# Layer norms of a two-layer kernel: eps on VectorE, one power first, additions behind the normalizations, a new order of phases

## The chip, the cores and the metric

The kernel runs on one core of a Trainium2 chip. The metric is the device time of one execution in microseconds; the median of three runs of the kernel before is 268.06 us (267.25 to 268.32).

## The reference, cut to what matters

An attention layer A and an MLP-mixer layer B, one after the other, each inside a layer norm and a residual. S is 2048, D is 448, F is 1792.

```python
def _layernorm(x, eps=1e-5):
    return (x - mean(x)) / jnp.sqrt(var(x) + eps)

def _A_ref(x, wqkv, wo):            # 16 heads of 28, window of 8 keys, dilation 2
    q, k, v = split(x @ wqkv)
    logits = einsum("bhsd,bhswd->bhsw", q, k[idx]) * scale
    attn = softmax(where(mask, logits, -1e9))
    return einsum("bhsw,bhswd->bhsd", attn, v[idx]) @ wo

def _B_ref(x, w1, w2, w3, w4):
    h = gelu(_layernorm(x) @ w1)
    hs = concat(quarters of h shifted by -1, +1, -2, +2 rows) @ w2
    x1 = x + hs
    return x1 + gelu(_layernorm(x1) @ w3) @ w4

h  = x + _A_ref(_layernorm(x), wqkv, wo)
h2 = h + _B_ref(_layernorm(h), w1, w2, w3, w4)
```

## The kernel before, in words

The 2048 rows are worked in four blocks of 512 (t = 0 to 3), each of four tiles of 128 rows (il). The phases of a block are:

- N1: row statistics of the input on VectorE, the reciprocal root of variance plus eps on GpSimd, four normalizations on VectorE into a tile of `lntm`. This is norm kind 0.
- A1: 16 transposes on TensorE, evicted by ScalarE (`transposed`, line 422), and 48 matmuls for q, k and v.
- A2: four VectorE multiplications of q with shifted k (tile `qk_r`), 32 small matmuls that sum over a head (four run at a time), and the softmax on VectorE and ScalarE (`mx`, `ls`, `zs`, `rz`, `pb`). The weights are written to a scratch tensor in DRAM.
- A3: 16 DMAs read them back, broadcast over the partitions of each head (tile `av_r`, four buffers, 28 partitions of 8192 bytes by each DMA). Four VectorE multiplications with shifted v follow, 32 accumulating matmuls, the projection with wo and the residual (20 matmuls), and ScalarE's write back into `xin`.
- B1: two layer norms in one (kind 1). The first norm's factor `rs_y[0:4]` is needed by B2; the product of both, `rs_y[4:8]`, is what B1 normalizes with. Then transposes, w1 and GELU. `mrs` is mean times factor and is needed by B3 alone.
- B2: w2 on the shifted quarters (it needs the neighbouring blocks' B1), the residual into `xb` in f32, statistics, kind 2's root, four normalizations in f32. Behind each normalization a GpSimd addition puts `xin` onto the same row tile of `xb` (line 538 and the following).
- W3: 14 x 4 matmuls with GELU into `h3T` tiles. B3: 4 x 14 matmuls, a VectorE step that adds `xb` (`ost`), and the output DMA. "w3" in the list is the load of the W3 weights, which lie in the place of wqkv, so that it follows A1 3.

The order is not written into the phases. `PLAN` (line 13) lists phases by priority. Each operation is recorded by `add` (line 99) with its priority, an assumed duration and what it reads and writes. `schedule` (line 140) then places the operations: on each engine, of those ready within a small slack of the earliest, the one with the best priority, and so on, with buffers given out as they come free. Each engine then runs its own list in that fixed order (`emit_engine`, line 608; every instruction is issued at line 612). SP's queue issues all DMAs in its own fixed order too. `rstd` (line 403) holds the root's steps, `normalize` (line 418) one normalization.

Of the kernel before, what the change touches and what calls it, by code (L numbers as in the profile page):

```python
# [9 lines left out]
F32 = mybir.dt.float32  # L10

_LAST = {}
PLAN = "N1 0, A1 0, N1 1, A2 0, N1 2, A1 1, A3 0, B1 0, A2 1, A1 2, N1 3, A2 2, A1 3, A3 1, A3 2, B1 1, B2 0, w3 0, B1 2, A2 3, W3 0, A3 3, B1 3, B3 0, B2 1, W3 1, B2 3, B3 1, B2 2, W3 2, B3 2, W3 3, B3 3"


class _Pool:


    def __init__(self, name, view, n):
        self.name = name; self.view = view  # L20
        self.free = [(0.0, k, ()) for k in range(n)]


# [65 lines left out]
class _Sched:  # L89
# [6 lines left out]
        self.prio = 0  # L96
        self.live = {}

    def add(self, eng, meth, dur, lag=60.0, chan=None, nbytes=0, table=None, **kw):
        op = _Op(len(self.ops), self.prio, eng, meth, kw, float(dur), float(lag))  # L100
        op.table = table
        if chan is not None:
            op.is_dma = True; op.chan = chan; op.nbytes = nbytes
        reads, writes = [], []
        for k, v in kw.items():
            if isinstance(v, _View):
                if v.tile not in op.tiles:
                    op.tiles.append(v.tile); v.tile.left += 1; v.tile.ops.append(op)
                name, plo, phi, ivs, psum = _rects(v.ap(0))
                name = v.tile.key  # L110
            elif isinstance(v, bass.AP):
                name, plo, phi, ivs, psum = _rects(v)
            else:
                continue
            if psum:
                plo, phi, ivs = 0, 128, [(0, 1)]
            (writes if k in self.WRITE_KEYS else reads).append((name, plo, phi, ivs))
        pe = eng == "pe"
        for (sp, plo, phi, ivs) in reads:
            for e in self.live.setdefault(sp, []):  # L120
                if e[1] and e[2] < phi and plo < e[3] and any(e[4] < hi and lo < e[5] for lo, hi in ivs):
                    op.deps.add(e[0])
        for (sp, plo, phi, ivs) in writes:
            L = self.live.setdefault(sp, [])
            for e in L:
                if e[2] < phi and plo < e[3] and any(e[4] < hi and lo < e[5] for lo, hi in ivs):
                    (op.odeps if pe and e[1] and e[0].eng == "pe" else op.deps).add(e[0])
            L[:] = [e for e in L if not (plo <= e[2] and e[3] <= phi
                                         and any(lo <= e[4] and e[5] <= hi for lo, hi in ivs))]
        for (sp, plo, phi, ivs) in reads:  # L130
            self.live[sp].extend([op, False, plo, phi, lo, hi] for lo, hi in ivs)
        for (sp, plo, phi, ivs) in writes:
            self.live[sp].extend([op, True, plo, phi, lo, hi] for lo, hi in ivs)
        op.deps.discard(op); op.odeps.discard(op)
        self.ops.append(op)
        return op
# [3 lines left out]
    def schedule(self, dma_bw=190.0, dma_fixed=2000.0, table_load=1300.0):  # L140
# [18 lines left out]
        table = None  # L159
        for _ in range(n):  # L160
            best = None
            for e in engs:
                fr = free[e]
                cands = []
                for op in ready[e]:
                    st = max(rdy[op.idx], fr)
                    for t in op.tiles:
                        if t.slot is None:
                            if not t.pool.free:
                                st = None  # L170
                                break
                            st = max(st, min(t.pool.free)[0])
                    if st is not None:
                        cands.append((st, op))
                if not cands:
                    continue
                first = min(st for st, _ in cands)
                st, op = min((c for c in cands if c[0] <= first + self.SLACK[e]), key=lambda c: (c[1].prio, c[1].idx))
                if best is None or st < best[0]:
                    best = (st, op)  # L180
            if best is None:
                stuck = sorted((op.prio, op.idx, op.eng, op.meth, [t.key for t in op.tiles])
                               for e in engs for op in ready[e])
                raise RuntimeError("no instruction can be placed: %s" % stuck[:20])
            st, op = best
            ready[op.eng].remove(op)
            for t in op.tiles:
                if t.slot is None:
                    f = min(t.pool.free)
                    t.pool.free.remove(f)  # L190
                    t.slot = f[1]; t.before = f[2]
                op.deps.update(t.before)
            op.t0 = st
            if op.is_dma:
                free[op.eng] = st + op.dur
                dma_free = max(st + op.dur, dma_free) + op.nbytes / dma_bw
                op.t1 = dma_free + dma_fixed
            else:
                dur = op.dur
                if op.table is not None and op.table != table:  # L200
                    table = op.table; dur += table_load
                free[op.eng] = st + dur
                op.t1 = st + dur + op.lag
            for t in op.tiles:
                t.left -= 1
                if t.left == 0:
                    t.pool.free.append((max(o.t1 for o in t.ops), t.slot, tuple(t.ops)))
            order[op.eng].append(op)
            self.gorder.append(op)
            for ch in children[op.idx]:  # L210
                npend[ch.idx] -= 1
                rdy[ch.idx] = max(rdy[ch.idx], op.t1 if op in ch.deps else op.t0)
                if npend[ch.idx] == 0:
                    ready[ch.eng].append(ch)
# [52 lines left out]
def bass_sequential_preLN__sliding_local_dilated__mixer_s_mlp__prompt_kernel(  # L267
# [30 lines left out]
    with ExitStack() as es:  # L298
# [50 lines left out]
        def shifted(t, u, c):  # L349
            return bass.AP(AR, A_KV + t * KVB + (u * 4 + c) * KVW + PADK, [[A_END, KC], [64, 8], [-DIL, NW], [1, 64]])  # L350

        def mm(out_ap, lhsT, rhs, start, stop, n, share=1.0):
            return S.add("pe", "matmul", 2.5 + share * n / 2.4, 220.0, out=out_ap, lhsT=lhsT, rhs=rhs, start=start, stop=stop)
        def act(out_ap, in_ap, func, n, **kw):
            table = {ACT.Exp: "exp", ACT.Gelu_apprx_tanh: "gelu"}.get(func)
            return S.add("act", "activation", 185 + 0.82 * n, 80.0, table=table, out=out_ap, in_=in_ap, func=func, **kw)
        def dve(meth, n, mode=1.0, **kw):
            return S.add("dve", meth, (90 + n / mode) / 0.96, 120.0, **kw)
        def pool(meth, n, **kw):
            return S.add("pool", meth, 130 + n / 0.5, 60.0, **kw)  # L360
        def dma(chan, out_ap, in_ap, nbytes, dur=400.0):
# [36 lines left out]

        def ln_stats(kind, src_ap, i):
            dve("bn_stats", D, out=st6[:, i, :], in_=src_ap)  # L400
            dve("bn_aggr", 8, out=mv[:, kind, i, :], in_=st6[:, i, :])

        def rstd(kind, t):


            var4 = mv[:, kind, 4 * t:4 * t + 4, 1]
            n = 8 if kind == 1 else 4
            pool("tensor_scalar", 4, out=rs_x[:, kind, t, 0:4], in0=var4, scalar1=EPS, scalar2=None, op0=ALU.add)
            if kind == 1:
                pool("tensor_scalar", 4, out=rs_x[:, kind, t, 4:8], in0=var4, scalar1=1.0 + EPS, scalar2=EPS * EPS,  # L410
                     op0=ALU.mult, op1=ALU.add)
            S.add("pool", "tensor_tensor", 1000, 60.0, out=rs_y[:, kind, t, 0:n], in0=rs_x[:, kind, t, 0:n],
                  in1=mhalf[:, 0:n], op=ALU.pow)
            if kind == 1:
                pool("tensor_tensor", 4, out=mrs[:, t, :], in0=mv[:, 1, 4 * t:4 * t + 4, 0], in1=rs_y[:, 1, t, 0:4],
                     op=ALU.mult)

        def normalize(kind, t, il, col, out_ap, in_ap):
            dve("tensor_scalar", D, 2.0, out=out_ap, in0=in_ap, scalar1=mv[:, kind, 4 * t + il, 0:1],
                scalar2=rs_y[:, kind, t, col:col + 1], op0=ALU.subtract, op1=ALU.mult)  # L420

        def transposed(ln):
# [115 lines left out]
        def phase_B2(t):  # L538
# [8 lines left out]
                ln_stats(2, xb[t][:, il, :], i)  # L547
            rstd(2, t)
            ln = _Tile(P_ln)
            for il in range(4):  # L550
                i = 4 * t + il
                normalize(2, t, il, il, ln(lambda v, il=il: v[:, il, :]), xb[t][:, il, :])
                pool("tensor_tensor", D, out=xb[t][:, il, :], in0=xb[t][:, il, :], in1=xin[:, i, :], op=ALU.add)
            b2_a[t] = transposed(ln)

        h3 = {}
# [1 line left out]
        def phase_W3(t):  # L558
            a = b2_a[t]
            h3[t] = [_Tile(P_h3) for _ in range(NF)]  # L560
            for f in range(NF):
                b = _Tile(P_bank)
                for c in range(4):
                    mm(b(), w3_s[:, c, f * 128:(f + 1) * 128], a(lambda v, c=c: v[:, c, :]), c == 0, c == 3, 512)
                act(h3[t][f](), b(), ACT.Gelu_apprx_tanh, 512)

        def phase_B3(t):
# [86 lines left out]
```

## Time and profile before

| what | value |
|---|---|
| median of 3 runs | 268.06 us (267.25 to 268.32) |
| span of the profiled execution | 269.7 us |
| TensorE busy | 241.8 us |
| VectorE busy | 167.5 us |
| ScalarE busy | 112.8 us |
| GpSimd busy | 54.3 us |

The profile has one execution. Its span is the only time recorded of it; the median is that of other executions. Matmuls are pipelined and their ends are modelled, so that neighbouring rows overlap a little. PEclk is the granted TensorE clock as a share of 2.4 GHz: 1.00 is the full level, 0.50 is 1.2 GHz.

### The profile page before, as it was taken

What the parts mean: (1) busy time and instruction counts of PE and PEld (TensorE: products, weight loads), DVE (VectorE), ACT (ScalarE), POOL (GpSimd) and SP (SyncE); (2) the same over time, 40 slices, a digit from 0 to 9 for tenths busy, and PEclk for the clock granted to TensorE, in tenths of its full rate; (3) what the DMA queues carried; (4) which work ended last, traced back from release to release, by engine and by line L of the source; (5) the groups of instructions that cost most, each with busy time, mean ns of one, the idle gap of its engine ahead of it and who ended that gap; (6) DMA issues with size and microseconds to landing.
All of it is one profiled execution on the core that took longest, in us unless ns stands there. A gap on an engine that the chain in (4) does not pass through costs nothing.

```text
span 269.7 us, 3248 instructions
## 1 busy us (share of the span) xinstructions
PE 241.8 (90%) x1297; PEld 125.6 (47%) x1297; DVE 167.5 (62%) x234; ACT 112.8 (42%) x178; POOL 54.3 (20%) x87
## 2 busy tenths in 40 slices
PE   0599897998899999798489999999899998999995
PEld 0355352453445565354154555555345544445452
DVE  3449999589896998888877553354992243001122
ACT  1222663353254944240238771314277035612600
POOL 5102042004306000303913000031761026000000
PEclk9999998699799999889959999999999999999999
DMA  7990003999599679995006992010000110000201
GB/s 217 307 328 16 2 1 53 174 174 174 114 165 175 124 193 187 158 159 91 0 19 142 181 186 38 17 38 17 0 0 2 34 34 2 0 0 0 71 17 51
DMA packets 24367, 24.70 MB, mean 92 GB/s; under 512 B 1376, under 2 KB 23456, under 8 KB 24352
## 3 DMA queue, kind: packets, MB, share of 16 engines
q1 hardware_dynamic: 24352, 24.50, 43.7%
q8 instruction: 10, 0.16, 0.3%
q14 instruction: 5, 0.04, 0.1%
HBM read 22.13 MB, written 2.36 MB: 91 GB/s over the span
## 4 chain that ended last, share of the span: by engine, by line
PE 66%; DVE 20%; POOL 7%; ACT 3%; issue 1%; DMA 1%
PE ps L612 66%; DVE st L612 5%; DVE lntm L612 4%; POOL rs_y L612 4%; DVE av_r L612 3%; POOL rs_x L612 2%; ACT actT L612 2%; DVE qk_r L612 2%; DVE mv L612 2%; DMA xin<-in_A_x_dram 1%; DVE arena L612 1%; ACT xin L612 1%; DVE zs L612 1%; DVE ls L612 1%; DVE pb L612 1%
## 5 line engine op out<-in xcount | busy, mean ns | idle before, releaser
L612 PE MATMUL ps<-actT,arena 112*128 112x512 bf16 (+1 forms) x416 | 100.8, 395 | 2.2 <-ACT actT L612 2.2
L612 PEld LDWEIGHTS ps<-actT,arena 112*128 112x128 bf16 (+1 forms) x416 | 47.9, 118 | 48.4 <-issue 7.7
L612 ACT ACTIVATE actT<-ps 112x1024 bf16<-112x1024 bf16 (+1 forms) x40 | 32.8, 852 | 69.0 <-PE ps L612 69.0
L612 ACT ACTIVATE arena<-ps 112x512 bf16<-112x512 f32 x58 | 33.7, 599 | 31.7 <-PE ps L612 31.2
L612 ACT ACTIVATE h3T<-ps 128x512 bf16<-128x512 f32 x56 | 32.1, 599 | 33.8 <-PE ps L612 33.7
L612 PE MATMUL ps<-arena,h3T 128*128 128x448 bf16 x224 | 44.4, 352 | 0.0
L612 DVE SCALAR_TENSOR_TENSOR ost<-ps,mrs,arena 128x448 bf16<-128x448 f32 x16 | 10.7, 681 | 52.8 <-PE ps L612 52.3
L612 DVE TENSOR_TENSOR av_r<-av_r,arena 112x4096 bf16<-112x4096 bf16 x16 | 36.4, 2285 | 9.1 <-DMA av_r<-attn_p_scratch 9.1
L612 POOL TENSOR_SCALAR rs_x<-mv 128x4 f32<-128x4 f32 x16 | 11.3, 706 | 141.8 <-DVE mv L612 141.5
L612 PE MATMUL ps<-av_r,ident 112*112 112x512 bf16 x128 | 33.1, 411 | 6.2 <-DVE ls L612 4.6
L612 DVE TENSOR_TENSOR qk_r<-arena 112x4096 bf16<-112x4096 bf16 x16 | 36.0, 2279 | 0.0
L612 PEld LDWEIGHTS ps<-arena,h3T 128*128 128x128 bf16 x224 | 21.8, 98 | 20.0 <-ACT h3T L612 0.2
L612 PE MATMUL ps<-ident,lntm 128*112 128x128 bf16 x192 | 18.9, 238 | 10.3 <-DVE lntm L612 10.1
L612 PEld LDWEIGHTS ps<-av_r,ident 112*112 112x112 bf16 x128 | 17.8, 141 | 19.4 <-DVE ls L612 5.0
L612 DVE BATCH_NORM_STATS2 st<-xin 128x6 f32<-128x448 bf16 x32 | 19.3, 604 | 11.2 <-ACT xin L612 6.7
L612 PEld LDWEIGHTS ps<-ident,lntm 128*112 128x112 bf16 x192 | 15.3, 142 | 19.2 <-DVE lntm L612 16.0
L612 POOL TENSOR_TENSOR rs_y<-rs_x,mhalf 128x4 f32<-128x4 f32 (+1 forms) x12 | 18.7, 1562 | 1.0
L612 POOL TENSOR_TENSOR arena<-arena,xin 128x448 f32<-128x448 f32 x16 | 18.0, 1154 | 2.5 <-DVE lntm L612 2.5
L612 PE MATMUL ps<-wo_s,actT 112*128 112x448 bf16 x64 | 16.4, 353 | 1.4 <-ACT actT L612 1.4
L612 PE MATMUL ps<-actT,w_s 112*112 112x512 bf16 x64 | 16.7, 412 | 0.8 <-ACT actT L612 0.8
L612 DVE TENSOR_SCALAR lntm<-xin,mv,rs_y 128x448 bf16<-128x448 bf16 x32 | 10.6, 392 | 7.1 <-POOL rs_y L612 7.1
L612 DVE TENSOR_SCALAR lntm<-arena,mv,rs_y 128x448 bf16<-128x448 f32 x16 | 12.9, 866 | 2.5 <-POOL rs_y L612 2.4
(38 smaller groups left out, 126.6 us busy)
## 6 DMA issues: line engine op xcount, KB each, us to landing
av_r<-attn_p_scratch SPq DMA_DIRECT2D x64, 224.0 KB
arena<-in_B_w_dram SPq DMA_DIRECT2D x2, 1568.0 KB, 9.9
xin<-in_A_x_dram SPq DMA_DIRECT2D x4, 448.0 KB, 8.5
out_dram<-ost SPq DMA_DIRECT2D x16, 112.0 KB, 1.7
arena<-in_A_wqkv_dram SPq DMA_DIRECT2D x1, 1176.0 KB, 7.3
w_s<-in_B_w_dram SPq DMA_DIRECT2D x2, 392.0 KB, 9.5
attn_p_scratch<-pb SPq DMA_DIRECT2D x4, 128.0 KB, 1.7
wo_s<-in_A_wo_dram SPq DMA_DIRECT2D x1, 392.0 KB, 10.8
```

What stands on the lines that cost most here:

```text
L612: inst = getattr(eng, op.meth)(**op.kw)
```

## The change

The list of phases is rewritten. The addition of eps (for kind 1 also the product form of the second norm) goes from GpSimd to VectorE. For kind 1 the power over eight columns becomes two over four, and the one that B1's normalizations need is issued first. The GpSimd additions of B2 depend on all four normalizations of the block (`after`). Some assumed durations are changed (`ns`, the power's 1100). `P_h3.order` gives the `h3T` buffers out in order of their use, and the first matmul of each W3 tile holds its buffer (`hold`). The diff, cut to its core:

```diff
-PLAN = "N1 0, A1 0, N1 1, A2 0, N1 2, A1 1, A3 0, B1 0, A2 1, A1 2, N1 3, A2 2, A1 3, A3 1, A3 2, B1 1, B2 0, w3 0, B1 2, A2 3, W3 0, A3 3, B1 3, B3 0, B2 1, W3 1, B2 3, B3 1, B2 2, W3 2, B3 2, W3 3, B3 3"
+PLAN = "N1 0, A1 0, N1 1, A2 0, A3 0, N1 2, A1 1, A2 1, A3 1, A1 2, N1 3, A2 2, B1 0, B1 1, B2 0, A1 3, A3 2, w3 0, A2 3, W3 0, B1 2, B2 1, B3 0, A3 3, B1 3, B2 2, W3 1, B3 1, B2 3, W3 2, B3 2, W3 3, B3 3"
...
-    def add(self, eng, meth, dur, lag=60.0, chan=None, nbytes=0, table=None, **kw):
+    def add(self, eng, meth, dur, lag=60.0, chan=None, nbytes=0, table=None, after=(), hold=None, **kw):
...
+        op.deps.update(after)
...
+        if hold is not None:
+            op.tiles.append(hold); hold.left += 1; hold.ops.append(op)
...
+                            if t.pool.order and t.pool.order[0] is not t:
+                                st = None
+                                break
...
-            dve("bn_aggr", 8, out=mv[:, kind, i, :], in_=st6[:, i, :])
+            dve("bn_aggr", 8, ns=180.0, out=mv[:, kind, i, :], in_=st6[:, i, :])
...
             var4 = mv[:, kind, 4 * t:4 * t + 4, 1]
-            n = 8 if kind == 1 else 4
-            pool("tensor_scalar", 4, out=rs_x[:, kind, t, 0:4], in0=var4, scalar1=EPS, scalar2=None, op0=ALU.add)
+
+            def power(lo):
+                S.add("pool", "tensor_tensor", 1100, 60.0, out=rs_y[:, kind, t, lo:lo + 4], in0=rs_x[:, kind, t, lo:lo + 4],
+                      in1=mhalf[:, 0:4], op=ALU.pow)
+
             if kind == 1:
-                pool("tensor_scalar", 4, out=rs_x[:, kind, t, 4:8], in0=var4, scalar1=1.0 + EPS, scalar2=EPS * EPS,
-                     op0=ALU.mult, op1=ALU.add)
-            S.add("pool", "tensor_tensor", 1000, 60.0, out=rs_y[:, kind, t, 0:n], in0=rs_x[:, kind, t, 0:n],
-                  in1=mhalf[:, 0:n], op=ALU.pow)
+                dve("tensor_scalar", 4, out=rs_x[:, kind, t, 4:8], in0=var4, scalar1=1.0 + EPS, scalar2=EPS * EPS,
+                    op0=ALU.mult, op1=ALU.add)
+                power(4)
+            dve("tensor_scalar", 4, out=rs_x[:, kind, t, 0:4], in0=var4, scalar1=EPS, scalar2=None, op0=ALU.add)
+            power(0)
...
-            dve("tensor_scalar", D, 2.0, out=out_ap, in0=in_ap, scalar1=mv[:, kind, 4 * t + il, 0:1],
+            return dve("tensor_scalar", D, ns=450.0 if kind == 2 else 330.0, out=out_ap, in0=in_ap, scalar1=mv[:, kind, 4 * t + il, 0:1],
...
+            nz = [normalize(2, t, il, il, ln(lambda v, il=il: v[:, il, :]), xb[t][:, il, :]) for il in range(4)]
             for il in range(4):
                 i = 4 * t + il
-                normalize(2, t, il, il, ln(lambda v, il=il: v[:, il, :]), xb[t][:, il, :])
-                pool("tensor_tensor", D, out=xb[t][:, il, :], in0=xb[t][:, il, :], in1=xin[:, i, :], op=ALU.add)
+                pool("tensor_tensor", D, after=nz, out=xb[t][:, il, :], in0=xb[t][:, il, :], in1=xin[:, i, :], op=ALU.add)
...
+            P_h3.order.extend(h3[t])
...
-                    mm(b(), w3_s[:, c, f * 128:(f + 1) * 128], a(lambda v, c=c: v[:, c, :]), c == 0, c == 3, 512)
+                    mm(b(), w3_s[:, c, f * 128:(f + 1) * 128], a(lambda v, c=c: v[:, c, :]), c == 0, c == 3, 512,
+                       hold=h3[t][f] if c == 0 else None)
```

## Rows read from the trace of the kernel before

**Rows 1.** The page's first line: the span.

```profile
span 269.7 us, 3248 instructions
```

**Rows 2.** Stages: from:to, length, busy us of each engine, granted clock, DMA share, GB/s.

```profile
70.00:90.00 20.00, 19.39 (x123) 10.64 (x122) 17.35 (x22) 11.50 (x19) 4.23 (x4) 0.95 0.94 166
...
42.38:142.16 99.78, 89.12 (x481) 46.95 (x482) 85.62 (x98) 43.22 (x69) 21.72 (x18) 0.90 0.74 132
142.16:266.89 124.73, 121.69 (x649) 61.82 (x647) 51.44 (x87) 53.23 (x87) 21.88 (x26) 1.00 0.20 44
```

**Rows 3.** Waits of TensorE from 42.3 to 142.16 us: total, times, longest.

```profile
PE ps L612 <- DVE ls L612: 4.6, 1, 4.6
...
PE ps L612 <- DVE lntm L612: 2.6, 3, 1.2
```

**Rows 4.** The chain that ended last, through B1 1 and B2 0: start, us, what.

```profile
106.08 0.55 ACT xin L612
...
122.12 0.69 DVE arena L612
...
123.47 2.19 DVE av_r L612
...
125.84 2.19 POOL rs_x L612
...
128.10 2.93 POOL rs_y L612
...
131.06 3.21 DVE lntm L612 x4
```

**Rows 5.** Waits of TensorE from 142.2 us on: total, times, longest.

```profile
PE ps L612 <- DVE lntm L612: 2.9, 5, 0.6
```

**Rows 6.** Stretches at half clock, columns as in rows 2.

```profile
45.00:51.40 6.40, 6.40 (x24) 2.35 (x28) 6.08 (x6) 1.95 (x3) 0.00 (x0) 0.50 0.93 152
68.70:72.20 3.50, 3.50 (x9) 1.82 (x10) 2.63 (x5) 0.00 (x0) 0.83 (x1) 0.51 0.34 90
112.80:116.50 3.70, 3.66 (x9) 1.91 (x10) 3.63 (x6) 1.50 (x2) 0.00 (x0) 0.54 1.04 152
135.60:139.20 3.60, 3.55 (x9) 1.88 (x10) 3.46 (x7) 0.63 (x1) 0.55 (x1) 0.50 0.00 0
```

**Rows 7.** GpSimd in order of time: start, us, instruction.

```profile
20.07 0.23 POOL L612 TENSOR_SCALAR rs_x<-mv 128x4 f32<-128x4 f32 x1 [11.23 <-DVE mv L612]
20.38 1.04 POOL L612 TENSOR_TENSOR rs_y<-rs_x,mhalf 128x4 f32<-128x4 f32 x1
...
107.59 0.50 POOL L612 TENSOR_SCALAR rs_x<-mv 128x4 f32<-128x4 f32 x2 [22.24 <-DVE mv L612]
108.17 1.67 POOL L612 TENSOR_TENSOR rs_y<-rs_x,mhalf 128x8 f32<-128x8 f32 x1
...
131.65 4.50 POOL L612 TENSOR_TENSOR arena<-arena,xin 128x448 f32<-128x448 f32 x4 [0.63 <-DVE lntm L612]
```

**Rows 8.** VectorE's durations: busy and mean ns by form, or ns min/median/max by tile.

```profile
L612 DVE TENSOR_TENSOR av_r<-av_r,arena 112x4096 bf16<-112x4096 bf16 x16 | 36.4, 2285 | 9.1 <-DMA av_r<-attn_p_scratch 9.1
...
L612 DVE BATCH_NORM_AGGREGATE mv<-st 128x2 f32<-128x6 f32 x48 | 8.7, 181 | 1.4
...
L612 DVE TENSOR_SCALAR lntm<-arena,mv,rs_y x16: 505/866/1228, 131.1 to 223.8; 128x448 bf16<-128x448 f32 x16
```

**Rows 9.** SP's queue: block 1's broadcasts, and block 3's write of the weights.

```profile
68.53 13.51 SPq L612 DMA_DIRECT2D av_r<-attn_p_scratch  x16
...
139.90 0.34 SPq L612 DMA_DIRECT2D attn_p_scratch<-pb  x1
```

**Rows 10.** TensorE in order of time, saturated: W3, transposes, B3 of one block.

```profile
194.23 12.25 PE L612 MATMUL ps<-actT,arena 112*128 112x512 bf16 x56
206.31 1.06 PE L612 MATMUL ps<-ident,lntm 128*112 128x128 bf16 x16
207.21 10.76 PE L612 MATMUL ps<-arena,h3T 128*128 128x448 bf16 x56
```

More of the change, by code (lines that the diff above doesn't have):

```diff
@@ L12 @@
 _LAST = {}
-PLAN = "N1 0, A1 0, N1 1, A2 0, N1 2, A1 1, A3 0, B1 0, A2 1, A1 2, N1 3, A2 2, A1 3, A3 1, A3 2, B1 1, B2 0, w3 0, B1 2, A2 3, W3 0, A3 3, B1 3, B3 0, B2 1, W3 1, B2 3, B3 1, B2 2, W3 2, B3 2, W3 3, B3 3"
+PLAN = "N1 0, A1 0, N1 1, A2 0, A3 0, N1 2, A1 1, A2 1, A3 1, A1 2, N1 3, A2 2, B1 0, B1 1, B2 0, A1 3, A3 2, w3 0, A2 3, W3 0, B1 2, B2 1, B3 0, A3 3, B1 3, B2 2, W3 1, B3 1, B2 3, W3 2, B3 2, W3 3, B3 3"
 class _Pool:
     def __init__(self, name, view, n):
-        self.name = name; self.view = view
+        self.name = name; self.view = view; self.order = []
         self.free = [(0.0, k, ()) for k in range(n)]
@@ L188, in schedule @@
                 if t.slot is None:
+                    if t.pool.order:
+                        t.pool.order.pop(0)
                     f = min(t.pool.free)
@@ L350, in shifted, with mm @@
             return bass.AP(AR, A_KV + t * KVB + (u * 4 + c) * KVW + PADK, [[A_END, KC], [64, 8], [-DIL, NW], [1, 64]])
-        def mm(out_ap, lhsT, rhs, start, stop, n, share=1.0):
-            return S.add("pe", "matmul", 2.5 + share * n / 2.4, 220.0, out=out_ap, lhsT=lhsT, rhs=rhs, start=start, stop=stop)
+        def mm(out_ap, lhsT, rhs, start, stop, n, share=1.0, hold=None):
+            return S.add("pe", "matmul", 2.5 + share * n / 2.4, 220.0, out=out_ap, lhsT=lhsT, rhs=rhs, start=start, stop=stop, hold=hold)
         def act(out_ap, in_ap, func, n, **kw):
@@ L356, in act, with dve @@
             return S.add("act", "activation", 185 + 0.82 * n, 80.0, table=table, out=out_ap, in_=in_ap, func=func, **kw)
-        def dve(meth, n, mode=1.0, **kw):
-            return S.add("dve", meth, (90 + n / mode) / 0.96, 120.0, **kw)
+        def dve(meth, n, mode=1.0, ns=None, **kw):
+            return S.add("dve", meth, ns or (90 + n / mode) / 0.96, 120.0, **kw)
         def pool(meth, n, **kw):
```

## The prediction

> **What bounds the kernel now.** I read the span first [rows 1], then the span cut into stages by what TensorE does [rows 2], then what ended TensorE's waits in the middle stage [rows 3], and last the chain of work through it [rows 4]. The profiled execution spans 269.7 us [rows 1]; no other time of it is given, and it lies 1.6 us above the median of the runs, 268.06 us. I work out differences against the span and take them off the median.
>
> The stages differ. From 142.16 us on (the first matmul of W3 0) TensorE is busy 121.69 of 124.73 us at full clock [rows 2]: it is the bound there, and nothing but its own 2.9 us of waits for normalized rows [rows 5] is left to gain. From 42.38 to 142.16 us it is busy 89.12 of 99.78 us, so 10.7 us idle, and the granted clock is 0.90 [rows 2]. Four stretches, 17.2 us together, run at half clock (0.50 to 0.54) [rows 6], which costs some 8.5 us. So 19 us are lost there, because VectorE (85.62 of 99.78 us) and the broadcasts of the attention weights feed it: the longest wait, 4.6 us, is for ls [rows 3], VectorE's softmax difference, and it stood in VectorE's queue behind B2 0's normalizations [rows 4]. One question decides: does the change let TensorE reach W3 0, where it is saturated, with less lost before?
>
> **Part 1: eps on VectorE, one power first.** Before, a mean's end on VectorE is followed on GpSimd by an eps instruction of 0.23 us and a power of 1.04 us; for kind 1 two eps instructions (0.50 us) and a power of 1.67 us [rows 7]. After, eps is VectorE's. No VectorE instruction on 128x4 elements is in the trace; it is bounded by 0 and by the aggregation of 128x6, 0.18 us [rows 8], and I take 0.18, the nearest row. There are 12 blocks with kind 1 twice: 16 instructions, at most 2.9 us of VectorE. They wait for the last aggregation, which stands right before them in the same queue, so they hold up what follows by their own length only. Kind 1's chain goes from 2.17 to 0.18 + 1.04 = 1.22 us, a gain of 1.0; kinds 0 and 2 gain 0 to 0.2 where GpSimd is undisturbed. The second power and mrs of kind 1 (1.04 us and little more) follow on GpSimd, and B2 reads them only behind B1's transposes, matmuls and GELU, so they cost nothing while that cover stands.
>
> Where GpSimd meets a VectorE multiplication (2.28 us, [rows 8]) the gain is larger: in B2 0 the eps instruction took 2.19 us and the power 2.93 [rows 4], against 0.23 and 1.04 alone [rows 7]. Each sat out one multiplication. The eps part of that goes; the power can still be held once, so it is bounded by 1.04 and 2.93.
>
> **Part 2: additions behind the four normalizations.** One f32 normalization takes 505 ns alone and 1228 ns beside an addition [rows 8]; the four of a block took 3.21 us [rows 4]. Undisturbed, 4 x 0.505 = 2.0 us: 1.2 us saved per block, four blocks. The additions, 4.50 us per block on GpSimd [rows 7], now start some 1 to 2 us later; their reader is B3's last step, behind all of W3. What is queued behind them on GpSimd is the next block's power: due while they run, it waits up to 4.50 us. That goes into the new gaps below.
>
> The rows show normalizations slowed by additions, and GpSimd held by multiplications; no multiplication starts during an addition. The Trainium skill, Advanced Engine Details and Errata, section VectorE Performance Modes, says that VectorE's second SBUF port is shared with GpSimd and that the two block each other. By that rule the additions, once out of the way of the normalizations, would meet the next two-input multiplications instead; it becomes a rival below.
>
> **Part 3: the written order.** This is the largest part. The list now puts A3 0 and A3 1 directly behind their A2, and B1 0, B1 1, B2 0 ahead of A1 3, A3 2 and A2 3. W3 0 needs B2 0, which needs blocks 0 and 1 only; before, A3 2 and A2 3 went largely ahead of it. I estimate the new start of W3 0.
> - Block 1's broadcasts were issued from 68.53 us on [rows 9], behind block 0's. They are 16 x 229 KB = 3.67 MB by the code, and 166 GB/s were moved in that stage [rows 2]: 22 us, so 90.6 us in both kernels. Then one multiplication 2.3, eight accumulating matmuls 1.8 (0.219 each, [rows 10]), the projection and two evictions some 2.5, and 2.5 for queues: xin of block 1 is ready at 99.7 us. Before it was 106.63 [rows 4].
> - From there to the last tile of B2 0 it took 15.5 us (106.63 to 122.12, [rows 4]). Off go 1.0 for the power and 1.7 for the 3.7 us at clock 0.54 [rows 6]: 12.8.
> - From that tile to the first normalization it took 8.9 us (122.12 to 131.06). Now 3.7 less the multiplication wedged in (1.4), eps 0.18 and power 1.04: 2.7; with a multiplication wedged in and a held power 6.9. I take the middle, 4.8.
> - Normalizations 2.0. From their end to W3 0 it took 7.9 us (134.27 to 142.16), of which 1.8 was half clock [rows 6] and 1.4 the rest of the wait for ls: 4.7.
>
> Sum 24.3, so W3 0 starts at 124.0 instead of 142.16: **-18.2 us**. The weights w3 (1.6 MB, 9.7 us at that rate) behind block 2's broadcasts would land at 90.6 + 22 + 9.7 = 122.3, just in time.
>
> What was done before W3 0 comes after it now. A3 2 has 32 matmuls of 0.219 and 20 of 0.192 [rows 10], 10.8 us; A2 3 has 32, four at a time, 1.8 us: **+12.6**. If part of it still fits ahead, down to half, this is +6. In the late stage the waits for normalized rows fall by **-2.0** of their 2.9 us (0 to -2.9). New gaps in the longer saturated stage: 0 to 5 us, I take **+1.0**. Block 0's first chain at the start: **-0.1**. The change to h3's slots adds no instruction; I cost it at nothing, since the saturated stage had no such wait. Its cover is the other block's matmuls; without it, it lies within the 5 us.
>
> Sum -6.7 us: span 263.0, median **261.4 us**, 2.5% faster. The bounds give about 252 to 269.
>
> **Rivals.**
> 1. *Multiplications stay in the way.* The planner takes what is ready first: a multiplication of block 2 or 3 that is ready goes ahead of a normalization that still waits. For: one of 2.19 us did so before B2 0's last aggregation, and GpSimd's power remains held for 2.93 us [rows 4]. With eight of them wedged into the chain (18 us) W3 0 starts near 142 with the same work done before it, and only the late 2.0 us and one or two us of chain are gained: 264.5 to 268.5 us. Against: the new list ranks B2 0 ahead. Chance 0.20, half of it within 0.5%. This is also the case in which the change does not do what it says, since the power alone is not what the rows wait for.
> 2. *Slower: block 3 arrives late.* A2 3 now ranks behind A3 2. Before, its weights were written at 139.90 us [rows 9], and 66 us later came the transposes of the next to last block (206.31, [rows 10]). From 124 us TensorE has W3 0, B3 0, W3 1, B3 1 (46 us by [rows 10]), A3 2 and A2 3 (12.6), and some 8 of B1 2 and B2 1, until 191; A3 3, B1 3, B2 2 and B2 3 add about 23, until 214. If the write comes after some 150 us, each further us is one of idle TensorE; from 158 on the kernel is slower. At 162 it would be 273 us at half clock's toll of 1 to 2 us more. For: VectorE is full up to W3 0. Against: VectorE has 25 us of slack after 124 us. Chance 0.14.
> 3. *The port moves the loss.* The additions of B2 0 hold the multiplications of A3 2 and A2 3 by up to their 4.50 us [rows 7]. If that reaches TensorE: 265.9 us. For: the exclusion is seen in the rows one way. Against: after 124 us these multiplications are not urgent. Chance 0.07. By the skill's rule named above this is where the time would go.
>
> **How the numbers follow.** The forecast has 0.55, and 0.04 lies below 254 us, where half of A3 2 still fits ahead. A measurement of this kernel tells some 0.5%, 1.3 us, from no change, so faster means below 266.7: 0.55 + 0.04 + 0.10 + 0.07 = 0.76; within 0.5% 0.10; slower 0.14. The range 254 to 269 leaves out 0.04 below and about 0.15 above.
>
> **What would show it.** In the new profile the four f32 normalizations of a block take about 2.0 us together and none over 0.6; GpSimd has no eps instruction; W3 0's first matmul comes at 122 to 127 us; TensorE's idle time before it no longer shows a wait of 4 us for ls; half-clock stretches sum to under 10 us. The prediction is wrong if W3 0 starts after 138 us, if block 3's weights are written after 150 us, or if TensorE waits over 5 us in all behind W3 0.

## The result, and the profile after

The changed kernel takes 256.91 us (median of 4 runs, 256.52 to 258.85) against 268.18 us: ratio 0.9548 with a 95% interval of 0.9495 to 0.9600, 4.5% faster. The forecast was 261.4 us in a range of 254 to 269, so sign and range held, and the gain was almost twice the forecast 2.5%. On a second chip the kernel e6, which does the same work in the same order (see the experiments), took 257.33 against 270.46 us (0.9517, interval 0.9456 to 0.9578).

The profiled execution spans 256.9 us and was the longest of the four (258.85 us; a span lies 1.9 to 2.0 us below the time of its run), so the stages below are a little longer than usual. The kernel before ran at two levels on the other chips, at a mean granted clock of 0.96 or of 0.98 to 0.99 and some 2 us apart (269.6 to 271.7 and 268.2 to 269.2 us on one of them), and its profile, with 0.962 and a span of 269.7 us, shows the longer one, while the changed kernel's four runs have 0.98. So the two profiles overstate the gain by some 1.5 us: the spans differ by 12.8 us, the medians by 11.3. First the page: span, busy times, and the granted clock in 40 slices.

```profile
span 256.9 us, 3245 instructions
...
PE 234.7 (91%) x1297; PEld 123.7 (48%) x1297; DVE 165.6 (64%) x250; ACT 112.2 (44%) x178; POOL 62.1 (24%) x75
...
PEclk9999999599979999999999999999999999999999
```

VectorE has 16 instructions more (250 for 234), the eps instructions, and is busy 1.9 us less; GpSimd is busy 7.8 us more with fewer instructions, 75 for 87. The next fences show why.

The stages, as in [rows 2], from the first small sums of A2 1 to the first matmul of W3 0 and from there to the last one (in the kernel before these eight sums, 0.6 us, stand just ahead of the border at 42.38 us):

```profile
42.66:129.58 86.92, 81.47 (x465) 44.05 (x465) 77.43 (x94) 41.84 (x68) 23.90 (x13) 0.94 0.83 149
129.58:254.10 124.52, 123.15 (x676) 63.15 (x672) 57.66 (x105) 54.04 (x87) 27.88 (x25) 1.00 0.21 45
```

The whole gain lies in the middle stage: 86.92 us where it was 99.78, 12.9 less. The late stage is as long as it was (124.52 and 124.73 us), with 27 matmuls more in it (676 for 649). Two of the four half-clock stretches of [rows 6] are gone; these are the two that are left:

```profile
43.96:50.30 6.34, 5.76 (x30) 3.11 (x31) 6.16 (x6) 1.94 (x2) 0.00 (x0) 0.53 0.86 169
...
71.66:75.06 3.40, 3.40 (x8) 1.79 (x9) 2.56 (x5) 0.00 (x0) 0.81 (x1) 0.51 1.00 186
```

So TensorE's idle time in the middle stage fell from 10.7 to 5.5 us (86.92 less 81.47), and 9.7 us instead of 17.2 run near half clock, which gives back some 4 us more. Some of the latter may belong to the execution that was profiled and not to the kernel, as said above. The 16 matmuls fewer (481 to 465) are some 2 us by my rates; the rest of the 12.9 is not apportioned. The waits of TensorE in the two stages (engine, line, what ended it: total, times, longest):

```profile
PE ps L626 <- ACT actT L626: 2.4, 4, 0.8
PE ps L626 <- DVE qk_r L626: 2.2, 1, 2.2
PE ps L626 <- DVE av_r L626: 1.8, 2, 1.4
PE ps L626 <- DVE lntm L626: 1.2, 2, 0.7
```

```profile
PE ps L626 <- DVE lntm L626: 1.2, 1, 1.2
```

The 4.6 us for ls of [rows 3] is gone. The late stage waits 1.2 us for normalized rows instead of the 2.9 of [rows 5].

VectorE's new and changed instructions by form, and then GpSimd in order of time:

```profile
L626 DVE TENSOR_SCALAR lntm<-arena,mv,rs_y 128x448 bf16<-128x448 f32 x16 | 7.1, 507 | 2.3 <-POOL rs_y L626 2.3
L626 DVE TENSOR_SCALAR rs_x<-mv 128x4 f32<-128x4 f32 x16 | 2.3, 167 | 0.3
```

```profile
8.07 1.03 POOL L626 TENSOR_TENSOR rs_y<-rs_x,mhalf 128x4 f32<-128x4 f32 x1 [3.83 <-DVE rs_x L626]
...
40.50 2.98 POOL L626 TENSOR_TENSOR rs_y<-rs_x,mhalf 128x4 f32<-128x4 f32 x1 [2.51 <-DVE rs_x L626]
...
98.36 4.13 POOL L626 TENSOR_TENSOR rs_y<-rs_x,mhalf 128x4 f32<-128x4 f32 x2 [25.89 <-DVE rs_x L626]
...
120.86 1.01 POOL L626 TENSOR_TENSOR rs_y<-rs_x,mhalf 128x4 f32<-128x4 f32 x1 [8.23 <-DVE rs_x L626]
125.26 10.24 POOL L626 TENSOR_TENSOR arena<-arena,xin 128x448 f32<-128x448 f32 x4 [3.40 <-DVE lntm L626]
...
190.53 4.00 POOL L626 TENSOR_TENSOR arena<-arena,xin 128x448 f32<-128x448 f32 x4 [1.89 <-DVE lntm L626]
```

Every f32 normalization now takes about 0.51 us, none the 1.228 of [rows 8]. The power is still held wherever a multiplication starts beside it: 2.98 us at 40.50 where it takes 1.03 alone. At 98.36 the two powers of kind 1 take 4.13 together. Block 0's additions meet multiplications and take 10.24 us; block 2's, alone, take 4.00. That is where GpSimd's extra busy time comes from: it waits, and counts as busy.

SP's queue, as in [rows 9], and TensorE's first matmuls of W3 0:

```profile
68.22 13.09 SPq L626 DMA_DIRECT2D av_r<-attn_p_scratch  x16
...
94.68 12.91 SPq L626 DMA_DIRECT2D av_r<-attn_p_scratch  x16
107.64 1.03 SPq L626 DMA_DIRECT2D arena<-in_B_w_dram  x1
139.68 0.34 SPq L626 DMA_DIRECT2D attn_p_scratch<-pb  x1
```

```profile
129.58 0.61 PE L626 MATMUL ps<-actT,arena 112*128 112x512 bf16 x2
```

Block 1's broadcasts start at 68.22 us, as before (68.53), and block 3's weights are written at 139.68, as before (139.90). Between these two fixed points the work was packed differently: W3 0 starts 12.6 us earlier, at 129.58.

### The profile page after: what moved, and what is told of

Read it like the earlier page. It is cut to its first block, busy times and chain, and to the rows that moved or that the text cites. A ratio compares the mean times of both kernels' runs of the same rounds, so it can differ in the third digit from the quotient of the medians.

```text
span 256.9 us, 3245 instructions
## 1 busy us (share of the span) xinstructions
PE 234.7 (91%) x1297; PEld 123.7 (48%) x1297; DVE 165.6 (64%) x250; ACT 112.2 (44%) x178; POOL 62.1 (24%) x75
## 4 chain that ended last, share of the span: by engine, by line
PE 55%; DVE 18%; DMA 12%; SPq 5%; POOL 4%; ACT 3%; issue 1%
PE ps L626 55%; DMA av_r<-attn_p_scratch 10%; DVE av_r L626 5%; SPq L626 5%; POOL rs_y L626 4%; DVE st L626 4%; DVE qk_r L626 2%; ACT actT L626 2%; DVE zs L626 2%; DMA xin<-in_A_x_dram 2%; DVE mv L626 1%; DVE lntm L626 1%; DVE pb L626 1%; DVE rz L626 1%; DMA attn_p_scratch<-pb 1%
## 5 line engine op out<-in xcount | busy, mean ns | idle before, releaser
L626 PE MATMUL ps<-actT,arena 112*128 112x512 bf16 (+1 forms) x416 | 100.6, 391 | 2.0 <-ACT actT L626 2.0
L626 PEld LDWEIGHTS ps<-actT,arena 112*128 112x128 bf16 (+1 forms) x416 | 46.9, 116 | 47.3 <-issue 7.0
L626 POOL TENSOR_TENSOR rs_y<-rs_x,mhalf 128x4 f32<-128x4 f32 x16 | 26.7, 1676 | 107.4 <-DVE rs_x L626 107.4
L626 DVE TENSOR_TENSOR av_r<-av_r,arena 112x4096 bf16<-112x4096 bf16 x16 | 37.7, 2354 | 7.9 <-DMA av_r<-attn_p_scratch 7.9
L626 DVE TENSOR_TENSOR qk_r<-arena 112x4096 bf16<-112x4096 bf16 x16 | 36.7, 2321 | 0.4 <-PE ps L626 0.4
L626 POOL TENSOR_TENSOR arena<-arena,xin 128x448 f32<-128x448 f32 x16 | 24.3, 1550 | 12.5 <-DVE lntm L626 12.5
L626 PEld LDWEIGHTS ps<-ident,lntm 128*112 128x112 bf16 x192 | 16.2, 142 | 15.5 <-DVE lntm L626 10.5
L626 PEld LDWEIGHTS ps<-av_r,ident 112*112 112x112 bf16 x128 | 16.8, 135 | 14.0 <-DVE av_r L626 3.5
L626 PE MATMUL ps<-actT,w_s 112*112 112x512 bf16 x64 | 14.7, 380 | 0.8 <-ACT actT L626 0.8
L626 DVE SCALAR_TENSOR_TENSOR arena<-xin,rs_y,ps 128x448 f32<-128x448 bf16 x16 | 10.6, 662 | 7.1 <-PE ps L626 7.0
L626 PE MATMUL ps<-w_s,arena 112*128 112x448 bf16 x64 | 14.6, 352 | 0.0
## 6 DMA issues: line engine op xcount, KB each, us to landing
w_s<-in_B_w_dram SPq DMA_DIRECT2D x2, 392.0 KB, 10.2
```

The lines of the kernel that those rows point to most:

```text
L626: inst = getattr(eng, op.meth)(**op.kw)
```

## The experiments

Each ratio is to the kernel before on the same chip, with its 95% interval. The medians are of the runs that the ratio takes: two of four for e1 and e3, nine of ten for e2, all of the others.

| label | order of the instructions | eps, powers, additions | median us | ratio |
|---|---|---|---|---|
| e6_no_hold | changed | changed | 257.33 | 0.9517 (0.9456 to 0.9578) |
| e8_new_order_old_norms | changed | before | 264.47 | 0.9791 (0.9733 to 0.9848) |
| e9_old_order_new_norms | before | changed | 266.13 | 0.9839 (0.9788 to 0.9891) |
| e3_adds_free | changed | additions as before | 258.69 | 0.9595 (0.9505 to 0.9685) |
| e4_eps_gpsimd | changed | eps as before | 258.31 | 0.9584 (0.9519 to 0.9649) |
| e12_one_power | changed | powers as before | 258.32 | 0.9572 (0.9528 to 0.9615) |
| e1_old_list | planned anew | changed | 274.47 | 1.018 (1.005 to 1.031) |
| e2_new_list_alone | planned anew | before | 269.92 | 0.998 (0.994 to 1.002) |
| e11_old_durations | planned anew | changed | 259.55 | 0.9602 (0.9560 to 0.9645) |
| e10_power_first | planned anew | changed | 260.09 | 0.9622 (0.9571 to 0.9673) |
| e13_power_first_b | planned anew | changed | 259.34 | 0.9586 (0.9538 to 0.9634) |
| e14_power_first_n | planned anew | changed | 258.75 | 0.9589 (0.9517 to 0.9662) |

**The list or the edits?** The first two kernels exchange the list of phases alone.

```diff
 # e1_old_list: the changed kernel
-PLAN = "N1 0, A1 0, N1 1, A2 0, A3 0, N1 2, A1 1, A2 1, A3 1, ..."
+PLAN = "N1 0, A1 0, N1 1, A2 0, N1 2, A1 1, A3 0, B1 0, A2 1, ..."
 # e2_new_list_alone: the kernel before
-PLAN = "N1 0, A1 0, N1 1, A2 0, N1 2, A1 1, A3 0, B1 0, A2 1, ..."
+PLAN = "N1 0, A1 0, N1 1, A2 0, A3 0, N1 2, A1 1, A2 1, A3 1, ..."
```

> The changed kernel with the list of phases of the kernel before; the instructions and assumed durations are the changed ones. Theory A (the order brings most): 263 to 268 us, W3 0 starting after 135 us. Theory B (the shorter norms bring most, 1.0 us per kind-1 root, 1.2 us per block of f32 normalizations, and the 2.2 us that an eps instruction sat out): below 260 us, W3 0 starting before 133 us.

> The kernel before with the new list of phases alone; eps and one power of eight columns on GpSimd, additions interleaved. Theory A (the order brings most): 257 to 261 us. Theory B (the norms bring most): above 264 us, since each root behind a multiplication still costs 2 to 3 us more and W3 0 starts later than 138 us.

Theory A's times failed in both kernels; theory B's failed in e1 and held in e2 (269.92 us, above 264, and W3 0 later than 138 us). The edits with the old list are slower than the kernel before (1.018), and the new list without the edits is no faster (0.998). Neither exchange brings a gain, so neither theory explains the pair. In e2's stages W3 0 starts at 139.09 us, and its middle stage is nearly as long as before:

```profile
41.58:139.09 97.51, 88.67 (x472) 47.44 (x473) 82.62 (x91) 43.02 (x69) 23.83 (x18) 0.88 0.75 134
139.09:265.50 126.41, 123.36 (x658) 62.55 (x656) 54.98 (x93) 53.68 (x85) 24.48 (x26) 1.00 0.21 44
```

But exchanging the list does not isolate the order: the planner makes a new one from the list, the instructions and the assumed durations. e1 also keeps the new durations, the ordered h3 buffers and the hold, and which of them made it slow was not tried. The next kernels keep the order written out and change the instructions in it.

**One edit undone in the changed order.** After the planner has run, e3 drops the additions' extra waits, and e4 hands the eps instructions back to GpSimd, right before their powers.

```diff
 # e3_adds_free, behind the planner
+for op in S.ops:
...
+        for d in op.extra - op.real:      # the waits that "after" added
...
+                op.deps.discard(d); d.users -= 1
 # e4_eps_gpsimd, behind the planner
+for op in S.ops:
+    if op.meth == "tensor_scalar" and op.eng == "dve" and op.kw.get("scalar1") in (EPS, 1.0 + EPS):
+        op.eng = "pool"
...
```

> The changed kernel in the same order on every engine, but each addition waits for its own normalization only. If the additions cost through the shared port: two of a block's four f32 normalizations take 1.2 us again, the four 3.2 instead of 1.8 us; block 0's delay W3 0 by 1.4 us and block 1's lengthen TensorE's wait at 159 us from 1.2 to some 2.6 us: 258.5 to 261 us. If these waits are hidden: within 0.7 us of the changed kernel, 256.2 to 257.6 us.

> The changed kernel in the same order, but the eps instructions back on GpSimd right before their powers. If the eps instruction sits out one multiplication and the power the next: roots behind two multiplications in a row (block 3's N1, and B1 0, B1 1) take some 2 us more and W3 0 starts 3 to 6 us later: 260 to 264 us. If only its own 0.25 to 0.5 us counts, because the power is held in the changed kernel too: 257 to 259 us.

e4 at 258.31 us is where only its own length counts. e3's 258.69 lies just inside the band for a cost through the port. Its trace has that cost, but not where it was expected: the normalizations of blocks 0 and 1 stay at 1.8 us and W3 0 is not delayed (128.38 us), while those of blocks 2 and 3 take 3.2, and the stage behind W3 0 is 125.97 us, 1.4 more than the changed kernel's.

```profile
157.32 1.77 DVE L632 TENSOR_SCALAR lntm<-arena,mv,rs_y 128x448 bf16<-128x448 f32 x4
187.04 3.22 DVE L632 TENSOR_SCALAR lntm<-arena,mv,rs_y 128x448 bf16<-128x448 f32 x4 [1.12 <-POOL rs_y L632]
```

The intervals of both overlap with each other and with the changed kernel's, 0.9517: by the times, each edit alone is worth something between nothing and some 1.7%.

**Order and edits, crossed.** e8 has the changed order with all three edits undone; e9 the order before with all three made (eps right behind the last aggregation, the additions moved behind the fourth normalization). e6 leaves out the ordered h3 buffers and the hold; the planner writes the same instructions with the same waits as for the changed kernel, so that these two additions do nothing in this plan, and e6 is its repeat.

```diff
 # e6_no_hold: the changed kernel
-            P_h3.order.extend(h3[t])
...
-                       hold=h3[t][f] if c == 0 else None)
+                       hold=None)
 # e8_new_order_old_norms, behind the planner: e3, e4, and for kind 1
+first.kw["out"], first.kw["in0"], first.kw["in1"] = second.both      # columns 0:8
...
+S.gorder = [op for op in S.gorder if op not in gone]      # the second power
 # e9_old_order_new_norms, behind the planner of the kernel before
+op.eng = "dve"                          # eps, moved behind its last aggregation
...
+op.deps.add(d); d.users += 1            # each addition, on all four normalizations
```

> The changed kernel without the ordered h3 buffers and without the hold on the first matmul of a W3 tile. The planner writes the same instructions in the same order with the same waits on every engine, so both theories expect the time of the changed kernel, 256 to 259 us, and it serves as its repeat on this chip.

> The changed kernel's order on every engine, with all three instruction edits undone in it: eps on GpSimd right before the power, one power of eight columns for kind 1, each addition waiting for its own normalization only. Theory C (the order that planner, list and assumed durations make together brings the gain, and the edits cost little by themselves): 258 to 262 us. Theory D (the edits bring the gain, and the list alone brings none, as the list alone was the same as before): 266 to 271 us.

> The order of the kernel before on every engine, with all three instruction edits made in it: eps on VectorE right behind the last aggregation, two powers of four columns, the first-needed one first, additions behind all four normalizations. Theory C (the order brings the gain): 264 to 270 us, the one to two us of B1 1's root and some of B2's normalizations less than before. Theory D (the edits bring it): 257 to 263 us.

This gives the shares, within the noise. Against the kernel before, the order with old norms gains 2.1% (1.5 to 2.7), the edits in the old order 1.6% (1.1 to 2.1), both together 4.8%; so some 1.1% comes only with both. In the changed order the edits are worth 7.1 us (264.47 less 257.33), in the old order some 4.3 (270.46 less 266.13). The kernel before itself ran from 266.46 to 271.45 us on this chip, so the two single gains are less sure than the three times 257.33, 264.47 and 266.13, and which of them is the larger stays open. Neither theory holds whole: e9 lies in C's band, but e8 misses C's by 2.5 us and D's by 1.5. Each of the two also runs an order that was planned for the other instructions, which may cost it something. The stages of e8 and of e9:

```profile
41.59:131.51 89.92, 81.57 (x464) 43.81 (x465) 77.85 (x88) 41.86 (x68) 26.18 (x21) 0.94 0.80 144
131.51:259.00 127.49, 124.03 (x676) 62.84 (x672) 60.88 (x98) 54.24 (x87) 24.56 (x26) 1.00 0.20 44
```

```profile
42.82:139.63 96.81, 88.22 (x481) 46.25 (x481) 84.80 (x104) 42.93 (x68) 16.83 (x14) 0.91 0.75 137
139.63:261.50 121.87, 121.16 (x649) 61.81 (x647) 48.11 (x95) 53.26 (x87) 19.40 (x21) 1.00 0.21 45
```

The edits act in both stages. In the changed order W3 0 starts at 129.58 with them and at 131.51 without, and the late stage is 124.52 us with and 127.49 without. In the old order it is 139.63 and 142.16, and 121.87 and 124.73. How they act is seen in VectorE's waits for the roots over the whole span (total, times, longest), in the kernel before, e9, e8 and the changed kernel:

```profile
DVE lntm L612 <- POOL rs_y L612: 9.5, 8, 2.1
DVE lntm L642 <- POOL rs_y L642: 5.9, 6, 1.9
DVE lntm L657 <- POOL rs_y L657: 13.6, 9, 2.1
DVE lntm L626 <- POOL rs_y L626: 7.0, 7, 1.2
```

The edits take 3.6 us off these waits in the old order and 6.6 in the changed one; eps alone back on GpSimd (e4) has 11.3, one power of eight columns (e12, below) 10.2. To this come the normalizations: those of blocks 0, 2 and 3 take 3.2 us in e8 and 1.8 in the changed kernel. On GpSimd the same is seen in e8 at B1 0 and B2 0, beside the changed kernel's rows at 98.36 and 120.86:

```profile
96.22 2.45 POOL L657 TENSOR_SCALAR rs_x<-mv 128x4 f32<-128x4 f32 x2 [24.69 <-DVE mv L657]
98.75 1.67 POOL L657 TENSOR_TENSOR rs_y<-rs_x,mhalf 128x8 f32<-128x8 f32 x1
...
120.64 2.18 POOL L657 TENSOR_SCALAR rs_x<-mv 128x4 f32<-128x4 f32 x1 [11.36 <-DVE mv L657]
122.89 1.04 POOL L657 TENSOR_TENSOR rs_y<-rs_x,mhalf 128x4 f32<-128x4 f32 x1
124.56 6.55 POOL L657 TENSOR_TENSOR arena<-arena,xin 128x448 f32<-128x448 f32 x4 [0.63 <-DVE lntm L657]
```

In the changed order one instruction sits out the multiplication, the eps instruction (2.18 us for 0.23) or the power (2.98 for 1.03). So moving eps saves its own length and the hop there, not the multiplication; e4's difference from the changed kernel, 0.4 to 0.7%, is within the intervals. In the old order it saves more: at B2 0 both the eps instruction and the power sat out a multiplication [rows 4], and in e9 only the power does:

```profile
126.36 2.98 POOL L642 TENSOR_TENSOR rs_y<-rs_x,mhalf 128x4 f32<-128x4 f32 x1 [16.02 <-DVE rs_x L642]
```

From the start of B1 0's first root instruction to the last power's end it takes 4.2 us here; in the changed kernel the first-needed power ends 3.06 us after its start and 0.25 us of eps stand before it, 3.3.

**Each of the three once, then.** e12 undoes the split of the power alone.

```diff
 # e12_one_power, behind the planner of the changed kernel: for kind 1
+first.kw["out"], first.kw["in0"], first.kw["in1"] = second.both      # columns 0:8
...
+S.gorder = [op for op in S.gorder if op not in gone]      # the second power
```

> The changed kernel in the same order on every engine, with one power of eight columns for kind 1 in place of two of four; eps and additions as changed. If the three edits simply add, this one must bring what eps alone (+0.7%) and the additions alone (+0.8%) leave of the 2.7% between the new order with old and with new norms: 260 us or more. If it costs its own 0.64 us at B1 0 and B1 1 only: 257.5 to 259 us, and the rest is an interplay of the edits.

258.32 us is the second case, its own 0.64 us at B1 0 and B1 1. By the middles of the intervals the three single edits give 0.8, 0.7 and 0.5%, together 2.0, against 2.7 for all three. An interplay of some 0.7% is possible, but the intervals, half a per cent or more each way, and the two chips that these ratios come from don't settle it.

**The planner's durations.** e11 plans the changed kernel with the old assumed durations.

```diff
 # e11_old_durations: the changed kernel
-            dve("bn_aggr", 8, ns=180.0, out=mv[:, kind, i, :], in_=st6[:, i, :])
+            dve("bn_aggr", 8, out=mv[:, kind, i, :], in_=st6[:, i, :])
...
-                S.add("pool", "tensor_tensor", 1100, 60.0, ...)
+                S.add("pool", "tensor_tensor", 1000, 60.0, ...)
...
-            return dve("tensor_scalar", D, ns=450.0 if kind == 2 else 330.0, ...)
+            return dve("tensor_scalar", D, 2.0, ...)
```

> The changed kernel with the planner's old assumed durations (aggregation, power, normalizations); list and edits are the changed ones, the planner makes its own order. Theory C2 (the list gives its gain only together with durations that are near the measured ones, as the list alone gave none): 260 to 266 us. Theory C1 (list and edits suffice, the durations shift little): 256 to 259 us.

259.55 us (0.9602) lies just below the first band and just above the second: neither theory's numbers hold. The durations are worth 0.9% by the middles and 0 to some 2% by the intervals, and list and edits carry most of it. e2 and e8 run the same instructions from the same list, in orders planned for different norms, and 1.9% lies between them (on two chips). So that the list alone gave nothing has its cause in what the planner was told about the norms, instructions and durations together.

**Is the held power worth avoiding?** In the trace of the changed kernel TensorE idles and runs at half clock behind N1 2 (from 40.5 us) and N1 3 (from 69 us), right behind held powers. e10 forbids VectorE to start a multiplication between a block's eps and its normalizations; e13 does it for B1 and B2 only, e14 for N1 only.

```diff
 # e10_power_first, in the planner of the changed kernel
+                    if e == "dve" and op.dur > 2000 and pending:
+                        continue
...
+            if op.root is not None:
+                if op.root[0] == "eps":
+                    pending.update(op.root[1])      # the block's four normalizations
+                else:
+                    pending.discard(op)
 # e13_power_first_b: the rule for kinds 1 and 2; e14_power_first_n: for kind 0
```

> The changed kernel, planned again with one rule more: between a block's eps instruction and its four normalizations VectorE starts no multiplication of 112x4096, so that the power is not held by it. If the held powers (2.99, 2.98, 3.05 and 3.06 us instead of 1.03) cost what the trace shows behind them (TensorE's idle and half clock around 42 to 50 and 68 to 75 us, some 9 us): 250 to 255 us. If VectorE's multiplications set the pace and only move back by the 1.1 us per root that VectorE now idles: 257 to 262 us.

> The changed kernel planned again with the rule of the run with powers first, for kinds 1 and 2 alone: N1 stays as it was, no multiplication of 112x4096 between eps and normalizations of B1 and B2. If the loss there came from the N1 roots, whose multiplications feed TensorE early: 253 to 256.5 us, W3 0 before 128 us. If the multiplications set the pace in B1 and B2 too: 257 to 261 us.

> As the one before, for kind 0 alone: the rule holds for N1's roots and B1 and B2 stay as they were. If TensorE's idle and half clock behind the roots of N1 2 and N1 3 are real losses: 253 to 256.5 us. If VectorE's multiplications set the pace there: 257 to 261 us.

All three are in the bands of the second case, and none beats the changed kernel. The rule did what it was to do: N1 2's power in e10 takes 1.01 us, and the clock of its middle stage is 0.98 where the changed kernel has 0.94. W3 0 starts later all the same, at 132.22:

```profile
39.25 1.01 POOL L641 TENSOR_TENSOR rs_y<-rs_x,mhalf 128x4 f32<-128x4 f32 x1 [1.08 <-DVE rs_x L641]
...
121.39 14.66 POOL L641 TENSOR_TENSOR arena<-arena,xin 128x448 f32<-128x448 f32 x4 [1.90 <-DVE lntm L641]
```

```profile
43.02:132.22 89.20, 81.76 (x473) 43.48 (x473) 77.56 (x94) 43.22 (x69) 20.09 (x13) 0.98 0.81 147
132.22:255.00 122.78, 121.56 (x668) 62.31 (x664) 59.68 (x102) 53.34 (x85) 29.53 (x23) 1.00 0.20 46
```

The normalized rows of B2 0 were not late, though. They start at 119.53 us in e10 (118.48 in e13), where the changed kernel has 123.41. The planner then put the multiplications of A3 2, now put off, and their sums and projection ahead of W3 0:

```profile
119.53 1.78 DVE L641 TENSOR_SCALAR lntm<-arena,mv,rs_y 128x448 bf16<-128x448 f32 x4 [1.12 <-POOL rs_y L641]
124.36 1.93 PE L641 MATMUL ps<-av_r,ident 112*112 112x512 bf16 x8
126.98 1.93 PE L641 MATMUL ps<-av_r,ident 112*112 112x512 bf16 x8 [0.69 <-ACT actT L641]
```

So TensorE idles 7.4 us in that stage (89.20 less 81.76) against 5.5, in spite of the fuller clock. On VectorE there was also little to gain: behind a free power it idles 1.12 us (at 119.53 above), behind one held by a multiplication 0.90, as here in the changed kernel, and over the whole of e10 7.7 us against 7.0.

```profile
109.06 1.32 DVE L626 TENSOR_SCALAR lntm<-xin,mv,rs_y 128x448 bf16<-128x448 bf16 x4 [0.90 <-POOL rs_y L626]
```

What these runs show is that the rule, as this planner uses it, gains nothing. That VectorE's multiplications set the pace is not shown by them; the earlier rows with W3 0 straight behind them, in an order written out, were not tried.

## Why the prediction was right, and where it was not

**Bound and place: right.** By the traces TensorE is saturated behind W3 0 and starved before it, and the gain is the earlier start of W3 0. The fixed point was right too: xin of block 1 was forecast for 99.7 us, since the broadcasts do not move. ScalarE ends it at 100.6 (its four writes, 1.85 us together, start at 98.78).

**The path to W3 0: too short.** Forecast 124.0, with 122 to 127 as the sign of being right; measured 129.58, a miss. The term that failed is "from there to the last tile of B2 0", 12.8 us. Here are the steps on the chain through B1 0 and B1 1 (start, us, what), and the last tile's step on VectorE:

```profile
98.36 3.06 POOL rs_y L626
...
101.44 1.31 DVE lntm L626 x4
...
105.97 3.06 POOL rs_y L626
```

```profile
119.02 0.68 DVE L626 SCALAR_TENSOR_TENSOR arena<-xin,rs_y,ps 128x448 f32<-128x448 bf16 x1
```

It took 18.4 us (100.6 to 119.02). In the kernel before B1 0 was long done when block 1 arrived; in the new order both B1 roots run one behind the other. These are the statistics of block 1 on VectorE, the last of four in the kernel before and the first of four in the changed one:

```profile
106.65 0.63 DVE L612 BATCH_NORM_STATS2 st<-xin 128x6 f32<-128x448 bf16 x1
```

```profile
102.67 0.62 DVE L626 BATCH_NORM_STATS2 st<-xin 128x6 f32<-128x448 bf16 x1
```

Before, three of the four were done as the rows came, and the last aggregation ended 0.9 us behind the last row (107.50 less 106.63). Here VectorE first served B1 0's root and normalizations, and it ended 5.1 us behind (105.69 less 100.6): 4.2 of the 5.6 us that I was short. From there to the end of the power it took 3.3 us, with 3.06 for a power that a multiplication held and that I had taken at 1.04: 2.0 more. The way from the power to the last tile gave some 0.6 back. The remaining steps fit: 4.4 us from that tile to the first normalization at 123.41 (forecast 4.8), 1.8 for the four normalizations (2.0), 4.4 from there to W3 0 (4.7).

**The work moved behind W3 0: too much.** This is the term of the sum that was mis-sized most. I added 12.6 us for A3 2 and A2 3 and had half of that as the lower bound. The row at 128.52, ScalarE's four last writes of block 2 into xin, shows that A3 2 was whole before W3 0:

```profile
128.52 1.84 ACT L626 ACTIVATE xin<-ps 128x448 bf16<-128x448 f32 x4
```

Of A2 3's four groups of small sums the last three stand at W3 0's start or behind it. The late stage has 27 matmuls more, by the trace's counts 20 of A2 3's small sums and 8 of B2's with w2, and TensorE is busy 1.5 us longer in it (123.15 less 121.69). With 1.5 in place of 12.6 and -12.6 in place of -18.2 the sum is 5.5 us lower: a span of 257.5 for the measured 256.9, where I had 263.0. So two errors of opposite sign, 5.6 us on the path and 11.1 on the work behind it, offset each other in part. That they did, and that the time stayed in the range, was luck. The ranking in the list did not become the order: while VectorE and GpSimd worked through the B1 chain, the planner filled the gaps with A3 2. I had argued that very rule for rival 1, as a harm, and left it out of the main sum, where it is the gain.

**The base and the bounds.** I put the profiled execution 1.6 us above the median, but compared a span with a time; like for like it is some 3.5 us, and the 1.7 and 1.8 us that I took off for two half-clock stretches rest on that one execution. My bounds, all taken on the same side and with the 2.1 us each way of the middle step, add up to 251 to 269.5, not 252 to 269.

**Late stage: right in size.** Waits for normalized rows fell by 1.7 us (forecast 2.0), and the new gaps did not come. e9 shows the share of the edits cleanly, at the same matmul count: 121.87 for 124.73 us.

**Prices: right, but for the held power.** The eps instruction takes 0.167 us (taken 0.18), four f32 normalizations 1.8 us (2.0). A held power takes 2.98 to 3.06 us, just above my upper bound of 2.93.

**The rivals.** Rival 1, multiplications in the way, is there in the rows (four of them between 105.87 and 123.49 us, and the held powers), but its result is not: W3 0 starts 12.6 us earlier and not near 142. That the rule of e10, e13 and e14 brought nothing doesn't speak against it, since the planner spent the earlier rows otherwise. Rival 2 did not come: block 3's weights are written at 139.68 us, 10 us ahead of the point from which it would have cost. Rival 3, the port: the additions did move onto the multiplications. The section of the Trainium skill that I named speaks of VectorE's 2p instructions alone; the same page, Advanced Engine Details and Errata, names VectorE instructions with two SBUF inputs under Miscellaneous Facts, GPSIMD Details, and these multiplications are such. The trace agrees that they conflict, and adds who waits how long. Beside block 0's additions the multiplication of A2 3 takes this long, where 2.28 us is usual [rows 8]:

```profile
129.78 2.85 DVE L626 TENSOR_TENSOR qk_r<-arena 112x4096 bf16<-112x4096 bf16 x1 [0.19 <-PE ps L626]
```

That is 0.6 us on VectorE against 6.2 us on GpSimd (10.24 less 4.00), where nobody waits.

**The forecast as a whole** said that the order is the larger part and the edits the smaller. The crossed runs give 2.1 to 3.2% for the order (without and with the edits) and 1.6 to 2.7% for the edits: larger by half a per cent, which the intervals leave open. By the two runs with exchanged lists I would have had to say that neither is worth anything.

## What to carry to other kernels

When a planner writes the order, exchanging its input is not an experiment on one part: write the order out, and change the instructions in it. When a phase moves down a priority list, don't move its time down with it; ask first which gaps ahead of its new place it will fill. And removing a wait that looks costly in the trace pays only if the order lets the next engine use what then comes earlier; look at what stands ahead of it in that engine's queue.

## What the runs showed of the hardware that was not expected

- Multiplications of two bf16 operands in SBUF and GpSimd instructions hold each other up, unevenly. GpSimd sits the multiplication out: a power of 1.03 us takes 2.98 to 3.06, an eps instruction of 0.23 takes 2.18. A multiplication beside additions is stretched from 2.28 to 2.85 or 2.90 us, in e10 to 3.17 at most, while four additions go from 4.00 to 10.24, and in e10 to 14.66 us. In these rows a multiplication loses no more than one addition lasts (0.89 of 1.00 us).
- In these rows a power held by a multiplication costs VectorE no more idle time than a free one, 0.90 us against 1.12: the multiplication that holds it fills most of the wait.
- A power over eight columns takes 1.67 us and over four 1.03; two over four in a row take 2.0 to 2.2 undisturbed, so the split costs GpSimd 0.3 to 0.5 us and gives the first result 0.6 us earlier.
- The clock recovered without the time: e10's middle stage has a granted clock of 0.98 and is 2.3 us longer than the changed kernel's at 0.94, with TensorE idle for 7.4 us in it instead of 5.5.
